# Moving shift products, query products, statistics and a table load within a transformer block

## The chip, the cores and the metric

The kernel runs on one core of a Trainium2 chip. The metric is the device time of one execution in microseconds (us), the median over the executions of a kernel. One execution per kernel is recorded by the profiler; in the two executions that are compared below its span is 1.8 us shorter than its device time. PE is TensorE, DVE is VectorE, ACT is ScalarE, POOL is GpSimd.

## The reference, cut to what matters

```python
x = A_x                                                     # 2048 x 1024, bf16
mod = (silu(c) @ w_mod).reshape(1, 6, 1, -1)                # w_mod 1024 x 6144
sa, ca, ga, sb, cb, gb = (mod[:, n] for n in range(6))      # shifts, scales, gates
h = layernorm(x) * (1 + ca) + sa
x = x + ga * attention(h)      # 32 query heads, 4 key-value heads of 128; the last 512 keys; then @ wo
h = layernorm(x) * (1 + cb) + sb
return x + gb * ((silu(h @ w_gate) * (h @ w_up)) @ w_down)  # 3584 wide
```

## The kernel before

The rows of x are handled in two halves of 1024. For each half, 64 attention steps follow each other. One step makes the query of a step ahead, the scores of one (row block, head), their exponentials on ACT, and the product with V of the step before. In the first half the first 24 queries are plain products of eight matmuls; later ones come from a scheme with seven products in place of eight, in which DVE forms sums of weights and adds products together. Each engine works through its own queue in the order in which the program emits it: in the traces, work that stands behind a wait starts after it, even where it does not need what is waited for.

```python
def qproj(i, b=QB):                        # one query of the first 24
    qproj_mm(i, b, 0, DT)                  # PE: 8 matmuls 128x512 into bank QB
    T.op(DVE, ... tensor_copy(qT_s[qs], bank(b)))

def pv(i):
    ...                                    # PE: 32 matmuls 128x129
    T.op(DVE, ... reciprocal(...))         # 0.18 us
    T.op(DVE, ... tensor_tensor(o_s[os_], <PSUM>, rlb, MULT))   # 0.69 us

def ln_stats(t):                           # statistics of one tile of x, for the later layernorm
    stats(t, t % 2, 0)                     # DVE bn_stats, 0.69
    yield
    stats(t, t % 2, 1)                     # DVE bn_stats, 0.69
    aggr(t % 8, t % 2)                     # DVE bn_aggr, 0.21
    yield

# start of the kernel: the shift of the first layernorm, spread between query products
qproj_mm(4, QB0[4], 0, DT); q_raw(4)
mod_sa(0)                                  # 16 one-column products per weight block
... k_turn(0, BB) ...
mod_sa(1)
qproj_mm(5, QB0[5], 0, HK)
mod_sa(2); mod_sa(3)
T.op(DVE, ... tensor_copy(mod_bf[:, 0:DT], ...))     # the shift
qproj_mm(5, QB0[5], HK, HK + 2)
q_bias_mm(0, 2, BB)                        # 16 one-column products and a copy
q_shifted(0)
...

def pre0(i):                               # ahead of step i in the first half
    ...
    if i in (8, 9):
        for dt in range(DT if i == 8 else 0):
            modulate(hT[1], B_hT[1], dt, 0, 0, B_mode, x1_tiles)    # 8 DVE ops
    if i < 9:
        if 2 <= i < 8:
            qproj(i + 4)
    elif i + 3 < NDI:                      # NDI = 24
        qproj(i + 3)
    ...
    mods(i)                                # DVE: one column product of 1.2 us every 4th step, its copies
    if i == 26:
        bg.append(stats_task(2 * TPC, 2 * TPC))      # 8 tiles, one yield per step

for i in range(lo, hi + 2):                # the attention steps
    pre(i)
    q_first_half(sc, i)
    scores(i - 1)
    pv(i - 2)
    q_second_half(sc, i)                   # PE products; every 4th step an add on DVE that PE waits for
    tick(i)                                # DVE: sums of weights, a unit of wo among them
    run_bg(1)                              # one yield of the statistics

def unit_load(end, ahead=()):              # 512 KB of wo into one of two buffers
    T.op(Q_of[slot][0], ... dma_start(dst, src), reads=ahead, writes=[w.b_raw, w.b_s3])

def unit_sums(k):                          # 4 DVE sums; the fourth overwrites the raw weights
    for (o, a, b, rd, wr) in (..., (rf[:, 1536:2048], b22, b12, [R], w.b_s3)):
        T.op(DVE, ... tensor_tensor(o, a, b, SUB), reads=rd, writes=[wr])
    T.op(Q_of[slot][1], ... dma_start(dst, w.four), reads=[w.b_s3] + w.b_s, ...)   # store, 512 KB
```

`unit_load` writes a buffer whose last part the store of its earlier unit still reads (`w.b_s3`). A load of wo can therefore start only when that store has landed.

The softmax here doesn't subtract the row's maximum and nothing guards it: scores larger than these inputs give would overflow.

## Time and profile before

| | before |
|---|---|
| device time, median of the first 3 runs | 1157.38 us (1157.05 to 1158.17) |
| span of the profiled execution | 1156.2 us |
| PE busy | 1140.9 us |
| mean granted clock of 25 later runs in the experiments | 1.0 in 11, 0.997 to 0.999 in 14 |

The prediction below shows the rows of PE's timeline with its waits. One more view is needed: what stands in DVE's queue ahead of the longest of these waits, the one that ends at 148.61. This is the timeline of DVE of the kernel before: start, duration, line, operation, tiles, count; a bracket would give a wait ahead of the row.

```profile
143.12 0.88 DVE L953 TENSOR_TENSOR arena<-arena 128x512 f16<-128x512 bf16 x2
143.92 0.69 DVE L427 BATCH_NORM_STATS2 st<-x_res 128x6 f32<-128x512 bf16 x1
144.52 1.21 DVE L604 SCALAR_TENSOR_TENSOR arena<-arena 128x1024 bf16<-128x1024 bf16 x1
...
147.06 0.69 DVE L427 BATCH_NORM_STATS2 st<-x_res 128x6 f32<-128x512 bf16 x1
147.78 0.21 DVE L431 BATCH_NORM_AGGREGATE mv<-st 128x2 f32<-128x12 f32 x1
147.91 0.64 DVE L832 TENSOR_TENSOR arena<-ps,tmp 128x512 bf16<-128x512 f32 x1
```

The last row is the add that PE waits for. No row has a bracket: DVE is not waiting for anybody, it is late with work that nobody needs soon. The two statistics and the aggregate (0.69, 0.69, 0.21) are such work; the change moves them.

### The profile page before, as it was taken

Reading aid. Unit: us, or ns where it says so; the run is one execution under the profiler, and the core shown is the slowest. Engines: PE = TensorE matmul, PEld = TensorE weight load, DVE = VectorE, ACT = ScalarE, POOL = GpSimd, SP = SyncE. Lnnn points to the kernel's source line nnn. Section 1 sums busy time; section 2 is a strip of 40 time slices with the busy share of each in tenths; the row PEclk is TensorE's granted clock in tenths of the full one; section 3 lists DMA queues with packets and bytes.
Section 4 is the critical chain, followed back from the end, with each engine's and each line's share of the span. In section 5 each row is a group of like instructions: output and inputs, shape, how many; then the busy total and the mean of one; then the engine's idle time right before and its main releaser. Section 6 shows DMA issues by size and latency. Waiting matters only on the chain.

```text
span 1156.2 us, 17989 instructions
## 1 busy us (share of the span) xinstructions
PE 1140.9 (99%) x6928; PEld 586.0 (51%) x7013; DVE 825.8 (71%) x1649; ACT 532.0 (46%) x744; POOL 67.0 (6%) x137
## 2 busy tenths in 40 slices
PE   8999999999999999999999999999999999999999
PEld 5555556654446565656444444444444444444444
DVE  4777997747667777786657898777558777776536
ACT  4857787720127777787110354454110444444110
POOL 1100231000000111111000010000000000000000
PEclk9999999999999999999999999999999999999999
DMA  9779999986807998945774332423774423234443
GB/s 318 126 191 223 204 212 208 231 203 188 223 23 186 203 209 203 209 96 125 181 217 146 97 86 73 110 74 100 210 209 138 119 77 106 73 99 133 130 158 109
DMA packets 299572, 179.96 MB, mean 156 GB/s; under 512 B 140512, under 2 KB 288736, under 8 KB 299488
## 3 DMA queue, kind: packets, MB, share of 16 engines
q1 hardware_dynamic: 236512, 92.31, 37.4%
q10 hardware_dynamic: 54336, 55.05, 15.2%
q0 software_dynamic: 8640, 31.46, 8.8%
q8 instruction: 55, 0.90, 0.3%
q14 instruction: 29, 0.24, 0.1%
HBM read 125.96 MB, written 19.92 MB: 126 GB/s over the span
## 4 chain that ended last, share of the span: by engine, by line
PE 94%; DVE 2%; SPq 1%; issue 1%; DMA 1%; ACT 1%; DVEq 0%; ACTq 0%
PE ps L272 94%; DMA arena<-in_w_mod_dram 1%; ACT arena L802 1%; DVE arena L832 1%; DVE arena L903 0%; SPq L341 0%; SPq L364 0%; DVE st L427 0%; SPq L310 0%; SPq L400 0%; SPq L359 0%; DVE arena L849 0%; SPq L382 0%; DVE arena L1558 0%; DVE arena L683 0%
## 5 line engine op out<-in xcount | busy, mean ns | idle before, releaser
L272 PE MATMUL ps<-arena 128*128 128x512 f16 (+2 forms) x6715 | 1135.1, 330 | 11.7 <-POOL arena L420 2.2
L272 PEld LDWEIGHTS ps<-arena 128*128 128x128 bf16 (+1 forms) x6800 | 578.6, 98 | 563.3 <-DVE arena L832 7.3
L802 ACT ACTIVATE arena<-ps 128x1024 bf16<-128x1024 f32 x256 | 261.2, 1021 | 45.4 <-PE ps L272 33.6
L835 ACT ACTIVATE tmp<-ps 128x512 f32<-128x512 f32 x167 | 99.7, 597 | 296.9 <-PE ps L272 285.3
L903 DVE TENSOR_TENSOR arena<-arena 128x512 f16<-128x512 bf16 x328 | 133.2, 419 | 3.0
L832 DVE TENSOR_TENSOR arena<-ps,tmp 128x512 bf16<-128x512 f32 (+1 forms) x134 | 91.8, 685 | 50.6 <-PE ps L272 37.8
L835 ACT ACTIVATE nsc<-ps 128x512 f32<-128x512 f32 x84 | 50.1, 596 | 93.2 <-PE ps L272 90.9
L824 DVE TENSOR_TENSOR arena<-ps,rl 128x512 f16<-128x512 f32 x128 | 88.5, 691 | 4.5
L832 DVE TENSOR_TENSOR arena<-ps,nsc 128x512 f16<-128x512 f32 x84 | 57.3, 687 | 41.3 <-PE ps L272 30.0
L821 DVE RECIPROCAL rl<-ps 128x4 f32<-128x4 f32 x128 | 23.1, 181 | 75.7 <-PE ps L272 74.9
L1543 ACT ACTIVATE arena<-arena 128x512 f16<-128x512 f16 x84 | 49.9, 624 | 32.4 <-DVE arena L832 32.4
L1043 DVE TENSOR_TENSOR arena<-arena 128x2048 f16<-128x2048 f16 (+3 forms) x56 | 56.0, 1011 | 9.3 <-PE ps L272 8.8
L1119 DVE TENSOR_TENSOR tmp<-ps,tmp 128x512 f32<-128x512 f32 x32 | 22.1, 689 | 55.0 <-ACT tmp L835 45.4
L835 ACT ACTIVATE arena<-ps 128x512 f32<-128x512 f32 x16 | 9.6, 597 | 89.7 <-PE ps L272 89.7
L953 DVE TENSOR_TENSOR arena<-arena 128x512 f16<-128x512 bf16 x120 | 47.9, 420 | 1.2
L427 DVE BATCH_NORM_STATS2 st<-x_res 128x6 f32<-128x512 bf16 x58 | 39.6, 682 | 3.6 <-DMA x_res<-in_A_x_dram 3.4
L604 DVE SCALAR_TENSOR_TENSOR arena<-arena 128x1024 bf16<-128x1024 bf16 x32 | 38.9, 1216 | 0.0
L1558 DVE TENSOR_TENSOR arena<-arena 128x512 f16<-128x512 f16 x84 | 34.9, 416 | 0.6 <-DVE arena L832 0.5
L1120 DVE TENSOR_TENSOR tmp<-tmp,rowb 128x512 f32<-128x512 f32 (+1 forms) x49 | 33.6, 687 | 1.7
L441 DVE TENSOR_SCALAR nsc<-x_res,mv,rstd 128x1024 f16<-128x1024 bf16 (+1 forms) x30 | 16.2, 539 | 25.9 <-DMA arena<-nsc 25.9
L1121 DVE TENSOR_TENSOR arena<-tmp,x_res 128x512 bf16<-128x512 f32 (+1 forms) x33 | 22.3, 676 | 1.1
L832 DVE TENSOR_TENSOR arena<-ps,rowb 128x512 f16<-128x512 f32 x28 | 19.3, 689 | 3.9 <-ACT rowb L835 3.4
(85 smaller groups left out, 323.3 us busy)
## 6 DMA issues: line engine op xcount, KB each, us to landing
arena<-in_A_wq_dram SPq DMA_DIRECT2D x30, 512.0 KB, 5.3
arena<-wo_sum ACTq DMA_DIRECT2D x7, 2048.0 KB, 8.1
arena<-in_B_w_gate_dram SPq DMA_DIRECT2D x28, 512.0 KB, 4.0
arena<-in_B_w_up_dram SPq DMA_DIRECT2D x28, 512.0 KB, 4.9
arena<-wd_sum ACTq DMA_DIRECT2D x8, 1792.0 KB, 7.7
arena<-in_B_w_down_dram ACTq DMA_DIRECT2D x6, 1792.0 KB, 7.7
arena<-in_A_wo_dram POOLq DMA_DIRECT2D x16, 512.0 KB, 4.9
wo_sum<-arena POOLq DMA_DIRECT2D x16, 512.0 KB, 4.5
```

The lines of the kernel that those rows point to most:

```text
L272: T.op(PE, lambda: TE.matmul(out_ap, lhsT, rhs, start=start, stop=stop, skip_group_check=skip), reads=reads, writes=[bank_buf])
L427: T.op(DVE, lambda: V.bn_stats(st_[sl][:, hf * 6:hf * 6 + 6], x_res[:, t, hf * 512:hf * 512 + 512]), reads=[B_x[t]], writes=[B_st[sl]])
L604: T.op(DVE, lambda: V.scalar_tensor_tensor(mt[n % 2], mt[n % 2], 1.0, sc_row, op0=ALU.mult, op1=ALU.mult, accum_out=mcol[:, n:n + 1]), rea ...
L802: T.op(ACT, lambda: A.activation(ex_s[es][:, 2 * kp:2 * kp + 2, :], banks2(SCB + 2 * kp), AF.Exp, scale=att_scale), writes=[PB[SCB + 2 * k ...
L824: T.op(DVE, lambda: V.tensor_tensor(o_s[os_].rearrange("p (a b) d -> p a b d", a=2), psap(PVB * 512, [[512, 2], [130, 2], [1, P]]), rlb, A ...
L832: T.op(DVE, lambda: V.tensor_tensor(out, bank(ba), other, ADD), reads=[ob2], writes=[PB[ba], ob])
L835: T.op(ACT, lambda: A.activation(dst, bank(bk), AF.Copy), writes=[PB[bk], db])
L903: T.op(st, lambda: eng.tensor_tensor(o, a, b, op), reads=rd, writes=[wr])
L953: T.op(DVE, lambda: V.tensor_tensor(o, a, b, SUB), reads=rd, writes=[wr])
L1043: T.op(DVE, lambda: V.tensor_tensor(o, a, b, SUB), reads=rd, writes=[sb])
L1543: T.op(ACT, lambda: A.activation(o, s_, AF.Silu), reads=[sb], writes=[ob])
L1558: T.op(DVE, lambda: V.tensor_tensor(gu[blk][:, p, :], o, s_, MULT), reads=[sb, ob], writes=[B_gu[blk][p]])
```

## The change

Six moves; no arithmetic of the kernel is removed. A: the shift products are spread between query halves, the bias products split, two dummy matmuls added. B: queries 11 and 23 are made half in one step and half in the next, so that no step is without a query. C: the statistics of the second half of the rows start at step 44 in place of 26. D: those of the second attention half start three steps later. E: a dummy Silu in the output phase loads ACT's table before the feed-forward part needs it. F: the first feed-forward statistics start two rounds later.

```diff
-            qproj_mm(4, QB0[4], 0, DT)
+            mod_sa(0)
+            qproj_mm(4, QB0[4], 0, HK)
+            mod_sa(1)
+            qproj_mm(4, QB0[4], HK, DT)
             q_raw(4)
-            mod_sa(0)
 ...
-            mod_sa(1)
+            mod_sa(2)
             qproj_mm(5, QB0[5], 0, HK)
-            mod_sa(2)
             mod_sa(3)
 ...
-            q_bias_mm(0, 2, BB)
+            q_bias_mm(0, 1, BB)
             q_shifted(0)
 ...
+            q_bias_mm(1, 2, XB)
             q_shifted(1)
             for dt in range(HK):
                 shift(dt)
+            warm(2, QB)                              # A
 ...
-                if i in (8, 9):
-                    for dt in range(DT if i == 8 else 0):
-                        modulate(hT[1], B_hT[1], dt, 0, 0, B_mode, x1_tiles)
                 if i < 9:
-                    if 2 <= i < 8:
+                    if 2 <= i < 7:
                         qproj(i + 4)
-                elif i + 3 < NDI:
+                    elif i == 7:
+                        qproj_mm(ND - 1, QB, 0, HK)  # B: first half of query 11
+                    elif i == 8:
+                        qproj(ND - 1, k0=HK)         # second half and the copy
+                        for dt in range(DT):
+                            modulate(hT[1], B_hT[1], dt, 0, 0, B_mode, x1_tiles)
+                elif i + 4 < NDI:
                     qproj(i + 3)
+                elif i + 4 == NDI:
+                    qproj_mm(NDI - 1, QB, 0, HK)
+                elif i + 3 == NDI:
+                    qproj(NDI - 1, k0=HK)
 ...
-                if i == 26:
+                if i == 44:                          # C
                     bg.append(stats_task(2 * TPC, 2 * TPC))
 ...
-                if i == NI + 46:
+                if i == NI + 49:                     # D
                     bg.append(stats_task(0, 2 * TPC))
 ...                                                  # in o_hook1
+                if idx == 3 and j == 0:              # E
+                    T.op(ACT, lambda: A.activation(acc[:, 0:1], mhalf[:, 0:1], AF.Silu), ...)
 ...
-                if sc == 0:
-                    bg.append(stats_task(2 * TPC, 2 * TPC))
                 for r in range(FP + 1):
+                    if sc == 0 and r == 2:           # F
+                        bg.append(stats_task(2 * TPC, 2 * TPC))
```

## The prediction

> **What bounds the kernel now.** I read the page first, for which engine sets the time.
>
> ```profile
> PE 1140.9 (99%) x6928; PEld 586.0 (51%) x7013; DVE 825.8 (71%) x1649; ACT 532.0 (46%) x744; POOL 67.0 (6%) x137
> ```
>
> PE is busy for 1140.9 of 1156.2 us. The change removes no matmul, so it can win only PE's idle time, 15.3 us in all, and time in which PE runs at a low clock. About 5 us of the idle time are outside the change: 2.2 at the very start, 2.8 at the end (last matmul 1153.4, last work 1156.2). So 2% (23 us) is out of reach whichever way it goes, and the question is how many of some 10 us come back.
>
> Second, the timeline of PE, which prints the idle time ahead of a row and what ended it. These are the rows that the change aims at.
>
> ```profile
> 24.30 0.55 PE L272 MATMUL ps<-sc_bf,arena 128*128 128x1 bf16 x16 [0.44 <-DMA arena<-in_w_mod_dram]
> 27.12 1.49 PE L272 MATMUL ps<-arena 128*128 128x512 bf16 x3 [0.86 <-DVE arena L683]
> 51.76 44.35 PE L272 MATMUL ps<-arena 128*128 128x512 bf16 x358 [0.46 <-ACT arena L802]
> 96.80 3.41 PE L272 MATMUL ps<-arena 128*128 128x512 bf16 x32 [0.69 <-ACT arena L802]
> 107.94 13.30 PE L272 MATMUL ps<-arena 128*128 128x512 f16 x106 [0.23 <-DVE arena L832]
> 121.39 26.62 PE L272 MATMUL ps<-arena 128*128 128x512 f16 x212 [0.15 <-DVE arena L832]
> 148.61 17.02 PE L272 MATMUL ps<-arena 128*128 128x512 f16 x137 [0.61 <-DVE arena L832]
> 165.83 34.50 PE L272 MATMUL ps<-arena 128*128 128x512 f16 x275 [0.20 <-DVE arena L832]
> 497.55 2.64 PE L272 MATMUL ps<-arena 128*128 128x512 f16 x21 [0.34 <-DVE arena L832]
> 649.77 50.56 PE L272 MATMUL ps<-arena 128*128 128x512 f16 x232 [0.39 <-DVE arena L832]
> ```
>
> The bracket understates a wait, since the end of the previous matmul is modelled and drawn out. I therefore take the distance between two matmul starts less the 0.216 us that a 128x512 matmul takes in a dense run (1065.32 to 1076.11 in the chain of waits: 49 recorded matmuls and one missing, 10.79/50). So counted the stalls are 0.62 (51.76), 0.85 (96.80), 0.39 (107.94), 0.31 (121.39), 0.19 (at 134.5), 0.77 (148.61), 0.36 (165.83), 0.50 (497.55), 0.55 (649.77), 0.30 (at 668.6).
>
> Third, the windows view around the first attention step, for the clock (columns: span, PE, PEld, DVE, ACT, POOL busy and counts, clock, DMA share, GB/s).
>
> ```profile
> 23.00:26.40 3.40, 2.82 (x55) 1.58 (x52) 0.55 (x3) 0.10 (x1) 0.00 (x0) 1.00 1.13 330
> 26.40:29.80 3.40, 2.68 (x22) 1.43 (x24) 2.32 (x10) 2.41 (x3) 0.00 (x0) 0.50 1.07 360
> ```
>
> For 3.4 us PE runs at half clock, just when attention begins. "99% busy" hides this.
>
> Fourth, the chain of waits at the entry of the feed-forward part.
>
> ```profile
> 646.59 0.76 ACT L1543
> ...
> 647.88 0.63 ACT arena L1543
> 648.51 0.49 ACT nsc L835
> 649.03 0.70 DVE arena L832
> ```
>
> The first ACT piece is the table load ahead of the first Silu; it, the Silu, a snapshot and an add stand between PE and its next product.
>
> **What the Trainium skill says.** "TensorE: Matmul & The Clock Gate", section "Part 1: The HAM clock gate": the array runs at half clock after a window of about 3.4 us of low activity, at full after a busy one; the window is free-running. The trace agrees: 0.50 for 3.4 us, matmuls 0.43 apart there (27.12, 27.55) against 0.216. In the window ahead, matmuls of 128 columns or more streamed for 32% of it (my count); a window from 9.3 us with 51% had not lowered the clock. "ScalarE: Activation LUTs", section "What ACT_TABLE_LOAD costs": 1283 ns for a load plus about 1380 ns of drain. The trace shows the 1.28 us; no drain on top is seen (snapshot ends 646.57, Silu starts 647.88). "PSUM — Partial Sum Buffer", section "The four PSUM rules": an accumulation may stay open while other banks are written, so a query product may be cut in two. "Perfetto Trace Analysis", section "Identifying the Most-Contended Engine", warns that matmul busy time is a poor measure; here it hid the low clock.
>
> **The change part by part.**
>
> *A, start.* The 64 one-column products for the shift (16 per weight block) are spread between halves of queries 4 and 5; the bias products of queries 0 and 1 become two groups; two dummy matmuls follow. Work in front of the last shift block is the same set, only permuted, and that block waits for its weights, landed at 24.25 in the chain of waits. Blocks 0 to 2 land at 19.71, 21.07, 22.80 by the trace's landings; the new order asks for them at about 19.7, 21.0 and 22.6, so some 0.4 us of small waits appear and vanish before 24.25. Then: eight bias products instead of sixteen end 0.2 us sooner, so the copy of the bias goes from 25.98 to about 25.77, the shift of query 0 (0.48) from 26.17 to 25.95, and the first scores from 26.71 to about 26.5: 0.2. (A first matmul at 26.71 is missing in the trace; its weight load is there.) Clock: after the change the window 23.0 to 26.4 holds eight products (1.73) and most of two dummies (0.3), about 2.0 of 3.4 us or 59%, against 32%. That is above the 51% that kept the clock. Between 26.71 and 29.8 half clock cost 4 x 0.215 on the first scores, about 0.4 on the next two products, 0.1 on the rest: 1.35. But the window is free-running, and the three timed runs lie 1.1 us apart (1157.05 to 1158.17, the profiled one 1157.99), which I read as executions with and without it. Against the median I count half: 0.7.
>
> *B, queries 11 and 23 split.* A step costs PE 8 x 0.216 for the query, 4 x 0.216 for scores, about 0.9 for PV: 3.5, as the exponentials 3.50 apart show. A step without a query costs PE 1.75, while its two exponentials take 2 x 1.02 = 2.05; the backlog stops PE in the third score bank. With four matmuls in each of two steps each costs 2.64, over 2.05, so ACT keeps up. Saves 0.6 at step 8. There the query's copy (0.61) now precedes eight modulations of 0.33; the last ends about when the next query reads it, so 0.1 may return. At step 21, 0.65 to 0.7: DVE is full from 100.8 to 107.9 with sums and lands the stall at 107.94; that chain starts when the PV before it ends, about 0.65 earlier, so the gain passes through. Together 1.25.
>
> *C, statistics of the second half moved from step 26 to 44.* Two bn_stats of 0.68 and an aggregate of 0.21 per tile, eight tiles. Stalls at 121, 134.5, 148.6 and 165.8 sum to 1.63; without statistics DVE waited 0.80 for ACT ahead of the same add (at 174.5), so all four should go. But steps 44 to 59 have the same weight sums and the same 1.2 us column product every fourth step until about step 57. Statistics put 0.60 and 0.75 in front of that add; less the 0.80 and the slack of PE, some 0.25 of stall is left, at steps 48, 52 and 56 (at 60 the sums have ended): 0.65 returns. Net 1.0.
>
> *D, statistics in the second attention three steps later.* The stall at 497.55 has two bn_stats, a column product, a copy of modulation values and a row broadcast together; three steps later only the statistics are left, and steps 112 to 125 carry them today without a stall. 0.5.
>
> *E, Silu table early.* A dummy Silu in the output phase, where ACT waits up to 28.8 us. The load (1.28) and dummy (0.2) fit between snapshots 3.5 us apart. At the entry the load exceeds the stall, so the whole 0.55 goes.
>
> *F, feed-forward statistics two rounds later.* Three halves (1.9 us of DVE) stand in the chain just before the stall at 668.6; later rounds carry such halves today without one. 0.3.
>
> Sum: 0.2 + 0.7 + 1.25 + 1.0 + 0.5 + 0.55 + 0.3 = 4.5, so 1157.4 - 4.5 = 1152.9 us.
>
> **The rivals.** *DVE's debt only moves (C gives nothing):* for it, DVE work per four steps of 13.1 us is 10.0 to 10.2 without statistics from 177 to 217 (windows view), and about 3.15 comes on top, as at 123 (12.4); against it, the worst stall, 0.77, coincides with one-time work that steps 44 on lack. It would make 1153.9. *The clock falls all the same or one window later:* for it, one-column products and bias waits stay; against it, my 59%. It would make 1153.6. *Everything adds up and nothing returns:* C gives 1.63, the clock 1.35: 1151.6. *New early waits on the shift weights become the path:* against it, their last landing sets the end and stays; if a landing slips by 0.5 us, 1153.4.
>
> **Range and chances.** The first two rivals together give 1154.6, the third 1151.6, with part D or E a little larger 1151.2. Eight in ten: 1151.2 to 1154.7. A gain or loss over 2% has no source in the profile: chance of faster 0.01, within 2% 0.98, slower 0.01.
>
> **What would show it.** In the profile after: clock 1.00 throughout from 23 to 33 us with score matmuls 0.216 apart (A); no wait on ACT near 50 and 95 (B); no wait on DVE between 108 and 170, perhaps three of some 0.25 between 185 and 220 (C); none near 495 (D); the table load inside the output phase, near 590 to 610, and no wait near 646 (E); none near 664 (F). PE's busy time should hardly move. I am wrong if the clock still drops, if the stalls between 185 and 220 sum to 1.6, or if the waits vanish and PE stands still as long elsewhere.

## The result, and the profile after

The kernel after ran 1154.68 us (median of 6, 1154.12 to 1155.48). The kernel before, its first three runs included, had a median of 1158.12 over 6 runs (1157.05 to 1162.47). The ratio is 0.9965, with an interval from 0.9949 to 0.9981. A ratio here is the mean time of one kernel's fast runs over the mean of the other's in the same rounds, so it is not quite the ratio of the medians: it says 4.1 us where the first three runs and the new median say 2.7. The profiled span fell from 1156.2 to 1152.5, by 3.6 us, and these two traces are compared step by step below. The time is 1.8 us above the 1152.9 that was predicted.

PE's busy time hardly moved, as it should. This is the page's line of engines, after.

```profile
PE 1140.7 (99%) x6930; PEld 585.6 (51%) x7015; DVE 826.0 (72%) x1650; ACT 532.3 (46%) x745; POOL 66.5 (6%) x137
```

All rows of PE's timeline after that carry a wait, over the whole span. From 105.51 on each row runs on to the next wait; rows without a wait ahead of that are left out:

```profile
2.17 1.03 PE L272 MATMUL ps<-arena 128*128 128x512 bf16 x2 [2.17 <-POOL arena L420]
11.67 1.14 PE L272 MATMUL ps<-arena 128*128 128x256 f16 x9 [0.58 <-DVE arena L519]
105.51 38.64 PE L272 MATMUL ps<-arena 128*128 128x512 f16 x302 [0.23 <-DVE arena L835]
144.83 54.50 PE L272 MATMUL ps<-arena 128*128 128x129 bf16 x448 [0.68 <-DVE arena L827]
199.48 33.18 PE L272 MATMUL ps<-arena 128*128 128x512 f16 x265 [0.15 <-DVE arena L835]
232.97 916.75 PE L272 MATMUL ps<-arena 128*128 128x512 bf16 x4999 [0.31 <-ACT arena L805]
```

Of the ten rows that the prediction shows, one is left: 107.94, now 105.51, which the change does not touch. But two are new or different in kind. At 144.83 PE waits 0.68 for a product's division (line 827), where it had waited for the add of the worst stall. At 199.48 it waits for an add, where nothing had waited before. The waits at 2.17, 11.67 and 232.97 have their like in the kernel before (2.17, 0.67 and 0.31 at 2.17, 11.29 and 235.22).

The clock at the start, in the windows view of the kernel after (columns as in the prediction):

```profile
23.00:26.40 3.40, 3.29 (x57) 1.76 (x54) 1.30 (x4) 0.90 (x2) 0.00 (x0) 1.00 1.14 326
26.40:29.80 3.40, 3.40 (x30) 1.67 (x30) 3.22 (x12) 2.34 (x3) 0.00 (x0) 1.00 1.07 363
```

The second window now has a clock of 1.00 in place of 0.50. The table load has moved too; the timeline of ACT in the output phase and at the entry of the feed-forward part:

```profile
590.29 1.28 ACT L1489 ACT_TABLE_LOAD   x1
591.59 0.20 ACT L1489 ACTIVATE acc<-mhalf 128x1 f32<-128x1 f32 x1
...
644.56 0.63 ACT L1555 ACTIVATE arena<-arena 128x512 f16<-128x512 f16 x1 [0.76 <-DVE arena L835]
```

The load and the dummy end at 591.79, and the next snapshot follows at 593.13 after waiting 1.34 for PE, so the load costs nothing there. At 644.56 the Silu waits for its input, not for a table.

Where the 3.6 us came from can be read from the starts of the exponentials, one pair per attention step. The table gives the start after less the start before, from the two traces.

| up to | after less before, us | this stretch | part |
|---|---|---|---|
| exponential of step 1 | -1.42 | -1.42 | A |
| step 8 | -1.79 | -0.37 | B, query 11 |
| steps 21 to 24 | -2.43 | -0.64 | B, query 23 |
| step 60 | -2.25 | +0.18 | C, and a late load |
| steps 116 to 120 | -2.77 | -0.52 | D |
| end | -3.64 | -0.87 | E and F |

C, which was to bring 1.0, brought nothing in this execution. The chain of waits of the kernel after, just ahead of the stall at 144.83 (start, duration, what):

```profile
136.33 5.17 DMA arena<-in_A_wo_dram
141.50 0.02 issue
141.53 0.44 DVE arena L956
141.97 0.02 issue
141.99 0.42 DVE arena L956
142.41 1.16 DVE arena L604 x2
...
143.67 0.38 DVE rl L824
144.06 0.02 issue
144.08 0.70 DVE arena L827
```

A transfer heads the chain. DVE had to form two sums (line 956) of a block of wo that landed at 141.50, and waited 1.48 for it. Behind the sums in the queue stood a column product (line 604) and only then the division (lines 824 and 827) that frees the banks for PE's next product. The load had been issued at 136.33, when the store from the same buffer had landed (127.90 to 135.78). In the trace before, the corresponding load landed at 143.09 and the sum began at 143.12, with hardly any wait. It would be natural to say that DVE, with the statistics in its queue, was further behind there. The traces say otherwise. These are the exponentials of step 33 and the sums, first before, then after:

```profile
139.77 2.13 ACT L802 ACTIVATE arena<-ps 128x1024 bf16<-128x1024 f32 x2
...
143.12 0.88 DVE L953 TENSOR_TENSOR arena<-arena 128x512 f16<-128x512 bf16 x2
```

```profile
136.82 2.13 ACT L805 ACTIVATE arena<-ps 128x1024 bf16<-128x1024 f32 x2
...
141.53 0.88 DVE L956 TENSOR_TENSOR arena<-arena 128x512 f16<-128x512 bf16 x2 [1.48 <-DMA arena<-in_A_wo_dram]
```

Counted from these exponentials, DVE is ready for the sum after 3.23 in both (in the trace before it idles for 0.11, too short for a bracket), and the load lands after 3.32 before and after 4.68 after. The change did not make DVE come to this sum sooner; the load was later.

The timeline of DVE after, ahead of the new stall at 199.48:

```profile
195.04 0.69 DVE L427 BATCH_NORM_STATS2 st<-x_res 128x6 f32<-128x512 bf16 x1
195.64 1.21 DVE L604 SCALAR_TENSOR_TENSOR arena<-arena 128x1024 bf16<-128x1024 bf16 x1
...
197.93 0.69 DVE L427 BATCH_NORM_STATS2 st<-x_res 128x6 f32<-128x512 bf16 x1
198.65 0.21 DVE L431 BATCH_NORM_AGGREGATE mv<-st 128x2 f32<-128x12 f32 x1
198.77 0.65 DVE L835 TENSOR_TENSOR arena<-ps,tmp 128x512 bf16<-128x512 f32 x1
```

It is the same picture as before the stall at 148.61: statistics directly in front of the add. Counted by distances of matmul starts, as in the prediction, the stalls between steps 24 and 60 are these:

```
before: 0.31 (121.0)  0.19 (134.5)  0.77 (147.8)  0.36 (165.3)               sum 1.63
after:                              0.85 (143.8)  0.24 (175.8)  0.19 (185.8)
                                    0.31 (199.1)  0.19 (212.6)               sum 1.78
```

So C removed 1.63, put 0.93 at its new place, and 0.85 came from a late load: a loss of 0.15 by this count, 0.18 by the exponentials.

### The profile page after: what moved, and what is told of

Its sections match the earlier page's. It is cut to its first block, busy times and chain, and to the rows that moved or that the text cites. A ratio compares the mean times of both kernels' runs of the same rounds, so it can differ in the third digit from the quotient of the medians.

```text
span 1152.5 us, 17997 instructions
## 1 busy us (share of the span) xinstructions
PE 1140.7 (99%) x6930; PEld 585.6 (51%) x7015; DVE 826.0 (72%) x1650; ACT 532.3 (46%) x745; POOL 66.5 (6%) x137
## 4 chain that ended last, share of the span: by engine, by line
PE 96%; DVE 1%; DMA 1%; issue 1%; ACT 0%; POOL 0%; POOLq 0%; DVEq 0%
PE ps L272 96%; DMA wo_sum<-arena 1%; DMA arena<-in_A_wo_dram 0%; ACT arena L805 0%; DVE arena L835 0%; DVE arena L956 0%; DVE arena L827 0%; PE ps L276 0%; DVE arena L906 0%; DVE arena L852 0%; DVE arena L604 0%; DVE rl L824 0%; DVE rowb L627 0%; POOL arena L300 0%; DVE tmp L1117 0%
```

## The experiments

The theory after the result: A, B, D, E and F do what was worked out; C exchanges stalls for stalls, and a late load of wo takes what is left. Its rivals: the dummies of A are what holds the clock; C is worth nothing whatever the loads do; the loss is a chance of one execution. Twelve runs were made, on three chips, one of them of the changed kernel itself; each had its own runs of the kernel before, with medians of 1160.33 (7 runs), 1157.90 (7) and 1158.86 (11). "After" in a diff is the changed kernel. The medians of the kernel before differ by more than some of the effects, so I lean on distances within traces and use the times as a check. One measure serves throughout: from the exponential of step 24 to that of step 60, with the waits of DVE for loads of wo that the trace lists in the first attention half.

| kernel | statistics at | waits for wo, us (count) | step 24 to 60, us |
|---|---|---|---|
| before | 26 | none listed | 120.24 |
| e2_start_alone | 26 | 3.1 (2) | 121.56 |
| e5_fill_idle | 26 | 2.8 (1) | 122.36 |
| e8_late_parts | 26 | 3.8 (3) | 122.73 |
| e1_stats_back | 26 | 4.3 (3) | 124.77 |
| after | 44 | 1.5 (1) | 120.41 |
| e13_changed_again | 44 | 1.8 (1) | 120.37 |
| e4_no_dummies | 44 | 1.9 (2) | 120.77 |
| e6_split_6_2 | 44 | none | 119.52 |
| e9_unit_slack | 44 | none | 119.51 |
| e11_slack_stats_back | 26 | none | 119.97 |
| e3_tile_in_gap | in the gap | none | 118.56 |
| e10_gap_and_slack | in the gap | none | 118.56 |
| e12_norms_apart | in the gap | none | 118.55 |

Two things can be read from the ten traces whose loads are not freed (all but e9 to e12). For the sum of step 36, DVE is ready between 3.15 and 3.23 after the exponential of step 33 in all ten, wherever the statistics stand; the load lands anywhere from 0.9 (e3) to 4.7 (after). Its lateness does not come from C. And with the statistics at 26 four of five traces (e1, e2, e5, e8) have a wait of 1.7 to 3.0 for a load near 217 us, while none of the five others has. So C may spare a late load there; this was not tested, and what C is said to be worth below does not count it.

### e1_stats_back: C undone

```diff
-                if i == 44:
+                if i == 26:
```

> The changed kernel with the statistics of the second half back at step 26. Theory M (what I now hold from the two traces): the move is worth nothing in time, because its three stalls of 0.2 to 0.3 us reappear at steps 48, 52 and 56, and the stall at step 36 is set by the landing of a weight load that DVE's sums wait for, so it stays at about 0.8: time 1154.7 within 0.4. Theory P (the prediction): the move is worth 1.0, so 1155.7. Theory N: the statistics stand behind the late load in DVE's queue, so the step 36 stall grows to 1.5 us or more and the move was worth 0.7 to 1.5 all the same: 1155.4 to 1156.2, with the growth at step 36.

It ran 1155.91 us (median of 4, 1154.99 to 1159.88), ratio 0.9972 (0.9942 to 1.0001). The times do not tell it from the changed kernel. The profiled execution was the slowest of the four, and its trace shows why. First its timeline of DVE, then that of PE, then its windows:

```profile
218.72 0.88 DVE L956 TENSOR_TENSOR arena<-arena 128x512 f16<-128x512 bf16 x2 [2.97 <-DMA arena<-in_A_wo_dram]
```

```profile
220.26 5.90 PE L272 MATMUL ps<-arena 128*128 128x512 f16 x31 [2.29 <-DVE arena L835]
```

```profile
217.00:220.40 3.40, 1.11 (x7) 0.37 (x5) 1.61 (x5) 1.55 (x2) 0.00 (x0) 0.96 1.09 362
220.40:223.80 3.40, 3.40 (x12) 1.27 (x11) 1.62 (x4) 1.35 (x2) 0.56 (x1) 0.54 0.60 147
```

DVE waited 2.97 for a load of wo, PE stood for 2.45 by start distances, and the next 3.4 us had a clock of 0.54. So a late load can cost its stall and a stretch of half clock. That the stall caused the low clock is argued from the order of the two, not shown. Its mean clock of 0.997 holds a second stretch of 0.50, from 11.9 to 15.3, so the start of A does not rule out every drop. At step 36 theory N comes nearest: behind a wait of 0.54 for the load stand stalls of 0.42 and 0.83. As a test of C's worth the run is inconclusive; it drew attention to the loads.

### e2_start_alone: before, with A alone

The diff is part A of the change as shown above, on the kernel before.

> The kernel before with only the start changed (products for the shift between the halves of queries, bias products in two groups, two dummies). Clock theory: granted clock 1.00 from 23 to 33 us, second exponential 1.4 us earlier than in the kernel before (30.3 against 31.7), nothing given back, so 1.4 us less than before's 1158.1 of the same runs, 1156.7. Rival: the later stalls are set by transfers and by DVE, so the gain shrinks to under 0.5 by step 40 and the time is within 0.5 of before.

It ran 1158.61 (4 runs, 1157.60 to 1160.02), ratio 0.9992 (0.9963 to 1.0022): no gain that the time shows. The trace does show one. All four runs had a clock of 1.00. The distance from the copy of the shift to the exponential of step 1 was 5.23 (24.76 to 29.99), as after (25.03 to 30.26) and against 6.65 before (25.03 to 31.68). The exponential of step 1 started 1.69 earlier than before. Then two waits for loads of wo, 1.37 and 1.68, brought stalls of 0.35 and 1.17, and at step 60 the lead was 0.37. The interval of the ratio reaches from about 4 us faster to 2.5 slower, so the time can neither show nor exclude the 1.4 that was expected; this holds for e5 and e8 too.

### e3_tile_in_gap: one whole tile of statistics in the step after the add

```diff
-                if i == 44:
-                    bg.append(stats_task(2 * TPC, 2 * TPC))
+                if 29 <= i <= 57 and i % 4 == 1:
+                    bg.append(stats_task(2 * TPC + (i - 29) // 4, 1))
+                    stat2[0] = True
 ...                                     # after run_bg(1) of the step
+                    if stat2[0]:
+                        run_bg(1)
+                        stat2[0] = False
```

> The changed kernel with the same statistics spread out: one whole tile (two bn_stats and an aggregate, 1.35 us of DVE) in every fourth step from 29 to 57, in the step after which DVE waits 1.3 us for PE. Theory: a stall comes from what stands in front of one add in the fourth step, not from DVE's sum of work; then the stalls of 0.24, 0.19, 0.31 and 0.19 after 170 us are gone, step 36 keeps about 0.8, and the time is 0.9 under the changed kernel: 1153.8. Rival: DVE's total work per four steps decides; then stalls of the same sum stay and the time is 1154.7.

It ran 1153.63 (4 runs, 1152.57 to 1155.71), ratio 0.9948 (0.9921 to 0.9974). No statistics stand in front of the add now. DVE's timeline at the place of the stall at 199.48:

```profile
194.52 1.22 DVE L604 SCALAR_TENSOR_TENSOR arena<-arena 128x1024 bf16<-128x1024 bf16 x1
...
197.70 0.69 DVE L835 TENSOR_TENSOR arena<-ps,tmp 128x512 bf16<-128x512 f32 x1 [0.80 <-ACT tmp L838]
198.85 0.18 DVE L824 RECIPROCAL rl<-ps 128x4 f32<-128x4 f32 x1 [0.45 <-PE ps L272]
```

DVE now waits 0.80 for ACT's snapshot ahead of the add, so the add is as early as it can be, and PE has no stall between steps 28 and 60. The stretch from step 24 to 60 is 1.85 shorter than after, more than all the stalls of 1.78 there. It also shows no late load. Only one trace stands for that, and e9 and e10 take it up. A stall of 1.02 appeared at 571 in the second output phase, where the trace after has none.

### e4_no_dummies: after, without the two dummy matmuls

```diff
             for dt in range(HK):
                 shift(dt)
-            warm(2, QB)
```

> The changed kernel without the two dummy matmuls. Streaming in the window 23.0 to 26.4 is then eight products, 1.73 us or 51%, instead of about 59%. If the reordering alone holds the clock: clock 1.00, first scores about 26.46, time 1154.6. If the dummies are what holds it: clock 0.50 for 3.4 us after about 26.4, second exponential about 1.3 us later, 1156.0.

It ran 1155.36 (4 runs, 1154.68 to 1156.17), ratio 0.9961 (0.9936 to 0.9985). The clock was 1.00 in all four runs and the distance from the copy of the shift to the exponential of step 1 was 5.22. Four clean runs alone would not fell the rival, since e8, with the old order and no dummies, has 1.00 in all four too. A count in the traces says more (matmuls of 128 columns or more, 0.216 us per 512 columns): between 19.6 and 32.4 no stretch of 3.41 us in e4 streams for less than 51%, as in the trace after, while in e8 the lowest is 38% and the window ahead of the drop in the kernel before had 35%. So the new order keeps PE as busy without the dummies as with them.

### e5_fill_idle: before, with four dummies and no other change

```diff
             mod_sa(2)
+            warm(2, QB)
             mod_sa(3)
 ...
                 shift(dt)
+            warm(2, QB)
```

> The kernel before with its old order and only four dummy matmuls added in PE's idle time: two ahead of the last shift block (idle 0.44 us there) and two ahead of the first scores (idle 0.6). Clock theory: streaming in the window 23.0 to 26.4 rises from 32% to about 54%, so the clock is 1.00 in every run, where before shows under 1.00 in about half of its runs; second exponential about 1.3 us earlier than in before's profile relative to the landing of the last shift block (6.1 us after it instead of 7.4). Time 1.3 under those runs of before that had the drop, equal to those that had not. Rival: the old order itself keeps the array too idle, drops stay in about half of the runs.

It ran 1159.06 (4 runs, 1156.70 to 1160.32), ratio 0.9997 (0.9970 to 1.0024). The clock was 1.00 in all four, and the distance from the copy of the shift to the exponential of step 1 was 5.43 (25.24 to 30.67). Compare three cases: 6.65 with the low clock and the old order, 5.43 with the full clock and the old order, 5.23 with the full clock and the new order. The clock is thus worth 1.22 and the order 0.20. The windows of e5 lie almost as in the trace before (a boundary at 26.49 against 26.41), and the one ahead of the boundary streams for 61% in place of 35%: the dummies alone held the clock there. In the time the gain does not show: the trace has a wait of 2.8 for wo, with a stall of 2.25 at 217, and another stall of 1.25 at 576.

### e6_split_6_2: query 11 cut into six and two matmuls

```diff
-                        qproj_mm(ND - 1, QB, 0, HK)
+                        qproj_mm(ND - 1, QB, 0, DT - 2)
-                        qproj(ND - 1, k0=HK)
+                        qproj(ND - 1, k0=DT - 2)
```

> The changed kernel with query 11 cut six to two instead of four to four. Theory: the 0.44 us that PE loses at step 9 comes from the copy of query 11, which stands in front of the eight modulations; with the last two matmuls only, the copy comes 0.43 us earlier, the small waits of 0.11, 0.11 and 0.23 near 52 us shrink to under 0.1 in all, and the exponential of step 9 gains 0.35 over the changed kernel. Rival: the modulations wait for the transposes of the norm, not for the copy; nothing moves. Step 8 has then 2 x 0.216 + 1.75 = 2.2 us of PE work over 2.05 of exponentials, so no wait on ACT in either case.

It ran 1155.27 (4 runs, 1153.67 to 1158.96), ratio 0.9971 (0.9941 to 1.0001). Theory and rival were both wrong. After has two small waits near 52 us, of 0.11 each; the 0.23 in the expectation is a matmul record that is missing from the trace (its weight load stands at 53.05). They became 0.19 and four of 0.11, and from the exponential of step 4 to that of step 8 it took 12.90, as before (12.90), against 12.52 after. The longer first part moves the product with V of that step back, and with it the division that stands ahead of the copy and of the modulations in DVE's queue: the division starts 0.43 later and the copy 0.38 later than after, counted from the exponential of step 4. Four and four is the better cut. By chance this trace had no late load, and it gave the first reading of C without one: 119.52.

### e8_late_parts: before, with D, E and F

The diff is parts D, E and F as shown above, on the kernel before.

> The kernel before with only the three late parts: statistics of the second attention three steps later, Silu table early, feed-forward statistics two rounds later. By the local positions in the two traces: 0.5 between the exponentials 110 and 116, and 0.85 between the last attention step and 670 us; no wait of PE near 497, 649 and 668; 1.4 us less than before in time. Rival: part of it is taken back by DVE in the feed-forward rounds from 3 on, so that PE waits for DVE there and the time falls by under 0.8.

It ran 1157.41 (4 runs, 1156.71 to 1158.09), ratio 0.9985 (0.9960 to 1.0010). Against the trace before, the exponentials gain 0.51 between steps 112 and 116 (+1.46 to +0.95), and from step 120 to the end 0.89 are gained (+0.95 to +0.06). The stalls at 497, 649 and 668 are absent. The positive offsets come from 3.8 us of waits for wo earlier. So D, and E and F as a sum, are confirmed in the trace apart from all else. The old order of the start had a clock of 1.00 in all four runs here.

### e9_unit_slack: after, with the loads of wo freed from the stores

```diff
-                T.op(Q_of[slot][0], ... dma_start(dst, src), reads=ahead, writes=[w.b_raw, w.b_s3])
+                T.op(Q_of[slot][0], ... dma_start(dst, src), reads=ahead, writes=[w.b_raw])
 ...                                        # the fourth sum goes into a buffer of its own, s3x
-                             ..., (rf[:, 1536:2048], b22, b12, [R], w.b_s3)):
+                             ..., (s3x, b22, b12, [R], B_s3x)):
 ...
-                T.op(Q_of[slot][1], ... dma_start(dst, w.four), reads=[w.b_s3] + w.b_s, ...)
+                T.op(Q_sx, ... dma_start(dst[:, 0:512], s3x), reads=[B_s3x], ...)
+                T.op(Q_of[slot][1], ... dma_start(dst[:, 512:2048], w.four[:, 512:2048]), reads=w.b_s, ...)
```

The buffer of 1 KB a partition comes from packing the rows of V at 144 in place of 160 elements.

> The changed kernel with the load of the next weight block freed from the store of the block before in the same buffer (the fourth sum goes to a buffer of its own, the rows of V are 144 instead of 160 elements apart to make room, and the store is two transfers). Theory: the stalls of 0.35 to 2.5 us that come and go between executions (0.85 at step 36 in the profile of the changed kernel) are DVE waiting for such a load, which starts only when a store has landed; then no wait of DVE on these loads is left, the stall at step 36 is under 0.1, those of 0.24, 0.19, 0.31, 0.19 after 170 us stay, the time is about 0.8 under the changed kernel, 1153.9, and its runs lie closer together. Rival: the loads are late because the transfers are contended, not because they start late; the waits stay.

It ran 1153.66 (4 runs, 1153.37 to 1153.92), ratio 0.9953 (0.9924 to 0.9981). No wait for wo is listed, and PE's timeline has no wait to print from 107.81 to 230.21:

```profile
107.81 122.40 PE L272 MATMUL ps<-arena 128*128 128x129 bf16 x1000
```

By start distances the stall of 0.85 is gone and the stalls of C stay (0.24, 0.18, 0.31, 0.18). From step 24 to 60 it takes 119.51, which is 0.90 less than after. The times lie within 0.55 us of each other, against 1.36 for the changed kernel's first six runs. The load for the sum of step 36 now starts at 129.03, beside the store (128.50 to 132.90) and not behind it, and lands at 135.99. One trace without a late load would prove little, since e3 and e6 have none either; but none of the four traces with freed loads has a wait, against seven of the ten others. So the chain from store to load is what makes the waits. The new packing of V was not run by itself.

### e13_changed_again: the changed kernel once more

> The changed kernel unaltered, on the same chip as the next three, to pair them. If late weight loads come and go between executions, its profile differs from the first one in the stall at step 36 (0.85 there) and nowhere else by more than 0.1 between the first and the last attention step; its runs spread over 1.5 us or more; median 1154.7 within 0.5.

It ran 1154.73 (6 runs, 1154.04 to 1155.71), ratio 0.9959 (0.9944 to 0.9975), as at first. But the late load had moved. DVE's timeline:

```profile
168.12 0.88 DVE L956 TENSOR_TENSOR arena<-arena 128x512 f16<-128x512 bf16 x2 [1.84 <-DMA arena<-in_A_wo_dram]
```

The stall of PE, 0.82, is at 170.0 in place of 143.8; the stalls of C are where they were, to 0.01. So the stall is not a property of step 36. It is a load that comes late at one step or another. It appeared in both traces of the changed kernel and in that of its near copy e4, though not in that of e6, so it is frequent rather than a chance of one execution.

### e11_slack_stats_back: e9 with the statistics at step 26

```diff
-                if i == 44:
+                if i == 26:
```

> Freed loads, and the statistics of the second half back at step 26: the move by itself without the stalls that come and go. Theory M (moving exchanges equal stalls): stalls of 0.31, 0.19, at most 0.5 and 0.36 at steps 28, 32, 36, 40 against 0.24, 0.19, 0.31, 0.19 after the move, so 0.1 to 0.45 slower than with freed loads and the move, 1153.7 to 1154.1. Theory P (the prediction's 1.0): 1154.7.

It ran 1154.13 (5 runs, 1153.61 to 1154.38), ratio 0.9953 (0.9936 to 0.9970). With no late load in either, the stalls are 0.31, 0.19, 0.51 and 0.36 (sum 1.37) with the statistics at step 26, and 0.24, 0.18, 0.31 and 0.18 (sum 0.91) at step 44. From step 24 to 60 it takes 119.97 against 119.51. In these two traces C by itself is worth 0.46, neither nothing nor 1.0; the ratios of the times are 0.9953 for both and do not resolve it. The stall at step 36 is 0.51 here and 0.77 before, though the same statistics stand there. Counted from the exponential of step 33, the sum that needs the load starts at 3.35 before and at 3.15 here, the add at 8.14 and 7.88; e2, with the statistics at 26 and no wait at this step, has 3.15, 7.88 and a stall of 0.51 as well. So 0.26 of the worst stall of the kernel before was a late load already, of a kind that no bracket shows.

### e10_gap_and_slack and e12_norms_apart: what follows from these, put together

e10 joins the edits of e3 and e9. e12 adds this in the norm of the output phase, against the stall at 571:

```diff
                 for tt in range(TPC):
                     norm_turn(ch, tt, tiles)
                     yield
-                for _ in range(3):
-                    yield
+                    if tt > 0:
+                        yield
+                yield
```

> The two experiments that gained, together: statistics as whole tiles in DVE's gap, and weight loads freed from the stores. If they act on different stalls they add: no stall of PE over 0.1 between steps 25 and 60, attention 0.93 (0.24 + 0.19 + 0.31 + 0.19) shorter than with freed loads alone, time 1152.7. Rival: with a tile in the gap DVE reaches the sums later and the loads were not late then anyway, so the time is that of one of them, 1153.6.

> As the gap-and-slack kernel, with the norm turns of the output and feed-forward phases two hooks apart instead of one. In five profiles of eight PE stood 0.25 to 1.25 us near 571, where DVE waits for the transpose that still reads the buffer of the norm before last. If that wait is what delays the residual sums, there is no stall of PE near 571 and the time falls by 0.2 to 0.8 under the gap-and-slack kernel. Rival: the modulations, now sooner after the last norm, wait for its transpose instead, and the stall comes back near 580 to 590.

e10 ran 1152.45 (6 runs, 1152.16 to 1153.89), ratio 0.9941 (0.9925 to 0.9957); e12 1152.45 (6 runs, 1152.05 to 1152.93), ratio 0.9940 (0.9923 to 0.9957). In e10 PE has no stall over 0.1 us between 107 and 231 and one of 0.58 at 571; PE's timeline:

```profile
106.47 464.90 PE L272 MATMUL ps<-arena 128*128 128x512 f16 x3400 [0.22 <-DVE arena L835]
571.78 577.51 PE L272 MATMUL ps<-arena 128*128 128x512 f16 x2686 [0.42 <-DVE tmp L1130]
```

In e12 the stall at 571 is gone, and one row runs from 105.34 to PE's end:

```profile
105.34 1042.25 PE L272 MATMUL ps<-arena 128*128 128x512 f16 x6086 [0.23 <-DVE arena L836]
```

Its span is 1150.4, but the median time is that of e10, so by time the last edit is worth nothing that these runs resolve. Both beat the changed kernel by 2.3 us (1154.73) and the kernel before by 0.6%.

## Why the prediction was right or wrong, point by point

**A, start: right in mechanism, half counted in size.** The prediction gave the new order 0.2 and the lost clock 1.35, and charged half of the latter against the median. Measured: order 0.20 (5.43 to 5.23, e5 and e8 against after), clock 1.22 (6.65 to 5.43). The profiled execution before had the drop, so in the traces A is the whole 1.42. Over the 25 runs of the kernel before that the experiments brought, 14 had a mean clock below 1, which fits the half but does not show it: some of these drops may lie elsewhere, as both of e1's did, and e8, with the old order, had none in four runs. The two dummies are not needed (e4).

**B: right, a little less.** 1.25 predicted, 1.01 measured, 0.37 at step 8 and 0.64 at step 21. At step 8 the copy of query 11 now stands ahead of the modulations and of the stall of 0.62 there 0.25 come back, over twice the 0.1 that was allowed. e6 shows that cutting elsewhere makes it worse.

**C: the step that failed.** The sum had 1.63 removed, 0.65 returned, 1.0 net; the traces before and after show -0.18. Two terms were mis-sized, and a third thing lies outside them.
First, the return was 0.93. (The prediction's own three stalls of 0.25 would already make 0.75.) At steps 48, 52 and 56 it is 0.69, but 0.24 come on top in the first group of steps. The prediction argued that the worst stall coincides "with one-time work that steps 44 on lack". Step 44 does not lack it: a copy of a broadcast row of 0.68 stands there at 173.27, ahead of the first statistics and the add. That this copy makes the 0.24 is argued from its place in the queue; no run takes it away.
Second, the statistics caused only 1.37 of the 1.63: 0.26 of the worst stall was a late load (e11). With the loads freed C is worth 0.46 (1.37 less 0.91, e9 against e11), and these two terms are what it lacks to 1.0.
Third, the 0.85 after is a late load of wo, for which the prediction had no term. It is not a cost of C: DVE is ready for that sum at the same place with and without it, and the same load is late in e1 and e8 with the statistics at step 26. So -0.18 is the luck of two executions, 0.26 of late load in the one and 0.85 in the other. Freeing and moving together save 0.73 against the kernel before (120.24 to 119.51).
The rival "DVE's debt only moves" came nearer in time than the main line, but its 1153.9 was still 0.8 too fast, and its claim that C gives nothing does not fit the 0.46.

**D: right.** 0.5 predicted, 0.52 measured, 0.51 in e8 alone.

**E and F: right.** 0.55 and 0.3 predicted, 0.87 together measured, 0.89 in e8. The load landed at 590.29, within the stretch that was named, and PE's busy time moved by 0.2 us.

**The sum.** With 1.42, 1.01, -0.18, 0.52 and 0.87 the traces give 3.64. The prediction's 4.5 counts half of the clock; with the whole of it, as in these traces, it would have been 5.15, so C's 1.2 is most of the miss, about half of it the two mis-sized terms and half the late load. That the range from 1151.2 to 1154.7 held 1154.68, at its very edge, is luck. It was built of the rivals, and none of them had a late load of wo.

**The signs that it named.** Clock 1.00 at the start, no wait on ACT near 50 and 95, none near 495, 646 and 664 and a table load near 590 all came true. For C, "no wait on DVE between 108 and 170" failed with the 0.68 at 144.83, and its last sign of being wrong came true in this trace: 1.63 of stalls vanished and PE stood still for 1.78 elsewhere.

**What stays open.** The kernel before varies from 1156.29 to 1163.5, and of its 25 runs in the experiments the 11 with a clock of 1.0 have a mean of 1157.65, the 14 others one of 1160.76. One drop at the start accounts for 1.22 of these 3.1 us. The rest could be late loads that stall PE long enough to cost clock as well, as in e1, where the wait near 217 that four of five traces with the statistics at 26 share came before a drop; no trace of a slow execution of the kernel before was taken that would show it. Nor was it found what makes one load take long and another not.

## What to carry to other kernels

In a kernel whose bound engine is 99% busy, count what stands in the helper engine's queue directly ahead of each operation that the bound engine waits for. Moving equal work to other steps of the same kind exchanged stalls here (1.37 for 0.91); moving it into the helper's own gap, the step behind that operation, removed them (e3, e10). Before putting a wait for a transfer down to a change, count from one and the same step when the engine was ready for it and when the transfer landed: here the engine was ready at the same place in ten traces, and the landing moved by 3.8 us. A load that may start only after a store has landed deserves a look at its slack, since one late load held up all that stood behind it in the queue. Where a transfer comes and goes between executions, one trace is not enough: the same kernel showed the same 0.8 us at two different steps.

## What the Trainium skill lacked or had wrong

- "TensorE: Matmul & The Clock Gate", section "HAM oscillation — how this bites in real kernels": the rule there is to avoid idle gaps of PE over about 3.4 us. Here the clock fell to 0.50 with gaps no longer than 0.86 us (the trace before). The page gives no share of activity that holds the clock. Each trace's own changes of clock mark off windows of 3.41 us. By the count of e4, windows that stream for 35% (before, from 23.0; the prediction counted 32), 34% (e1, from 8.5) and 33% (e1, from 216.7) are followed by 0.50; windows with 39% (e2, from 8.5), 41% (e5, from 217.6) and 48 to 51% (e12, before, e5, e8) are not. So a stall of 2.45 us cost clock in e1, and one of 2.25 us, which a boundary at 217.6 cuts in two, did not in e5.
- "ScalarE: Activation LUTs", section "What ACT_TABLE_LOAD costs": about 1380 ns of drain are to be added to each load. No such drain shows: 1.30 us lie from the snapshot's end (646.57) to the Silu (647.88) before, and 0.02 from the load's end (591.57) to the dummy (591.59) after.
- No page that I read names the pattern of the late loads: a load that waits for a store of its own buffer (7.88 us of store, 5.17 of load) and stands ahead of unrelated work in an in-order queue, where 1.48 us of waiting on DVE became 0.85 us of stall on PE.
- No page that I read says how far transfers of one size spread within one kernel: the 512 KB stores of wo took from 3.3 to 9.1 us in the first attention half of the traces before and after.
